# Turning the last two first blocks on quarters of the array, and converting v one head at a time

## The chip, the cores and the metric

The kernel runs on one core of a Trainium2 chip. The metric is the device time of one execution in microseconds (us), lower is better. Engine names are those of the profile: PE is the matrix engine, PEld its weight loads, DVE the vector engine, ACT the scalar engine, POOL the GpSimd engine, SP the engine that here only issues DMAs.

## What is computed

Attention with a forgetting gate over 8 batches, 8 heads, 576 positions and 64 numbers a head, and behind it a feed-forward layer on the 4,608 tokens:

```python
scores = scale * q @ k.T                                  # per batch and head, 576 x 576
cum    = cumsum(log(clip(f, 1e-4, 1)))                    # per batch and head
scores = where(causal, -1e9, scores + cum[:, None] - cum[None, :])
attn   = softmax(scores)
x      = (attn @ v), heads side by side                   # 4608 x 512
h      = x @ w_in                                         # 4608 x 2048
out    = (h * sigmoid(h)) @ w_out                         # 4608 x 512
```

The gate's factor of a key is put onto v: a row of v times its weight, with a column of ones beside it, so that one product gives both the numerator and the denominator of the softmax.

## The kernel before

**Blocks.** The 576 positions of a sequence are cut into a *first block* (128 rows), a *rest* (three blocks of 128) and a *tail* (64 rows). All engines' orders are written out by hand: an engine runs its instructions in the order of the calls in the source.

**First blocks.** For each batch `b`, `load_qk0(b)` (POOL's DMA queue, line 134) brings q and k of the first 128 rows as bf16 into one tile `qkb`, two DMAs a batch, each over all 128 partitions (16 runs of 8 rows, times 8 heads). `turn0(b, i)` turns q (`i` = 0) or k (`i` = 1) so that the 64 numbers of a head lie on partitions: 16 products on PE (line 293) with the loaded numbers as weights, 128 rows by 64 columns of the array, and a selection matrix `sel` as the moving operand, into a PSUM tile `tp` of the pool `pbig` (four buffers, shared with `hp`, `po`, `dn`, `tx`). ACT copies the turned q out, DVE the turned k (line 300). `scores0`, `mask0`, `out0` and `back0` do the attention of the block; score tiles come from the pool `psc` (tag "sc", two buffers). The function `two_more(b)` does the batches 4 and 5, later 6 and 7, with feed-forward work between its steps.

**Feed-forward work.** `m1_chunk` is the first product (PE line 583 into `hp`, then ACT's tanh, line 591, and DVE's product, line 592, into `gt`), `m2_part` a quarter of a second product (line 628 into `po`, four products of 512 columns), `m2_rows` the same on halves of the array's rows (line 654). `step(kind)` issues the next one; kind 1 is a chunk, kind 2 a part. `fill(us)` issues steps until about so many microseconds of PE time are used. They are what PE does between the attention's steps.

**Rest and tail.** 32 pairs of heads, `n` = 0 to 31, four a batch. q and k come in as float32 (`load_qk`, SP's queue; the second half of k straight into `qkb` by POOL's queue, line 160), `cast_qk` makes them bf16 on POOL (lines 409 and 413), `transposes(n)` turns them by a transposing DMA into `qkT` (SP's queue, line 443), `scores(n, c)` (PE line 475, then ACT's exponentials) and `mask`/`mask_tail` (DVE lines 492 and 498) follow, and `attend(n)` (PE lines 522 and 531) multiplies with v. `qkT` has four buffers. `turn(n)` casts, loads and turns three and four pairs ahead.

**v.** `load_v(b, c)` brings a block of v for all 8 heads as float32 into `vf`. `convert_v(b, c)` on POOL (line 429) multiplies it by the weights and writes bf16 into `vp`: one `tensor_tensor` over 8 heads of 65 columns (520), with the weight broadcast along the columns; the tail (`c` = 3) is two of 260 columns on 64 partitions. It is called for the next batch, `c` = 0 and 1 at the third pair of a batch, `c` = 2 and 3 at the fourth, after that pair's casts and k loads in POOL's order.

**The order around the change.** After the first four first blocks, POOL's order is: small fills, `load_w_out` 0 and 1, `convert_v0` of 4 and 5 (which wait for their v), `load_w_out` 2 and 3, `load_qk0` 6 and 7, `load_v0` 6 and 7, then the casts of the pairs. SP starts the loads of the pairs when `w_out`'s second quarter has landed. PE does `two_more(4)`, eleven steps in a written order of kinds, `fill(2.2)`, `two_more(6)`, `fill(4.2)`, and then the loop over the pairs.

Of the kernel before, what the change touches and what calls it, by code (L numbers as in the profile page):

```python
# [9 lines left out]
ALU = mybir.AluOpType  # L10
FP32 = mybir.dt.float32
BF16 = mybir.dt.bfloat16
P = 128
# [5 lines left out]
def kernel(  # L19
# [10 lines left out]
    nc = tc.nc  # L30

    B, H, S, D = q.shape
    DM, DFF = moe_w_in.shape
    BH = B * H
    NCC = DM // P
    NFC = DFF // P
    NP = H // 2
    SM = 512
    ST = S - SM
    NM = SM // P  # L40
    NR = NM - 1
# [6 lines left out]
    RUN = 8  # L48
    NRUN = P // RUN
    assert D == 64 and S == 576 and DM == H * D and NP == NCC and B == 8  # L50
    assert NRUN * H == P
    scale = 1.0 / float(D) ** 0.5

    ctx.enter_context(tc.manual_schedule(engines=set(ORDERED)))
# [1 line left out]
    const = ctx.enter_context(tc.tile_pool(name="const", bufs=1))  # L56
    stage = ctx.enter_context(tc.tile_pool(name="stage", bufs=1))
    conv = ctx.enter_context(tc.tile_pool(name="conv", bufs=6))
    qktp = ctx.enter_context(tc.tile_pool(name="qktp", bufs=4))
# [8 lines left out]
    psc = ctx.enter_context(tc.tile_pool(name="psc", bufs=2, space=bass.MemoryType.PSUM))  # L68
# [2 lines left out]
    w_in_bf = const.tile([P, NCC, DFF], BF16, name="w_in_bf")  # L71
    w_out_bf = const.tile([P, NFC, DM], BF16, name="w_out_bf")
    w_bf = const.tile([P, NM + 1, BH], BF16, name="w_bf")
    ident_bf = const.tile([P, P], BF16, name="ident_bf")
    sel = const.tile([P, 2, D], BF16, name="sel")
    ident_f = const.tile([BH, BH], FP32, name="ident_f")
    tri = const.tile([P, P], BF16, name="tri")
    trit = const.tile([P, 2, ST], BF16, name="trit")
# [3 lines left out]
    junk = const.tile([1, 16], BF16, name="junk")  # L82
    kT0 = [const.tile([P, NP, P], BF16, name=f"kT0_{b}") for b in range(B)]
    v0 = [const.tile([P, H, D + 1], BF16, name=f"v0_{b}") for b in range(B)]
    vps = [const.tile([P, NM, H, D + 1], BF16, name=f"vp_{i}") for i in range(2)]
    uts = [const.tile([P, NM + 1, 3, ST], BF16, name=f"ut_{i}") for i in range(4)]
    vfs = [const.tile([P, H, D + 1], FP32, name=f"vf_{i}") for i in range(4)]

# [41 lines left out]

    def load_qk0(b):
        t = conv.tile([P, 2, RUN * D], BF16, name="qkb", tag="qkb")
        for i, src in enumerate((q, k)):
            nc.gpsimd.dma_start(
                out=t[:, i, :],
                in_=src[b, :, 0:P, :].rearrange("h (r c) d -> r h (c d)", c=RUN),
            )
        qk0[b] = t

    def load_v0(b):  # L140
# [62 lines left out]
    def load_w_out(i):  # L203
        c0, c1 = i * NFC // WQ, (i + 1) * NFC // WQ
        nc.gpsimd.dma_start(
            out=w_out_bf[:, c0:c1, :],
            in_=moe_w_out[c0 * P : c1 * P, :].rearrange("(fc p) m -> p fc m", p=P),
        )
# [76 lines left out]
    def turn0(b, i):  # L285
        src = qk0[b]
        if i == 0:
            qT0[b] = qktp.tile([P, NP, P], BF16, name="qT0", tag="qT0", bufs=2)
        dst, evac = ((qT0[b], nc.scalar.copy), (kT0[b], nc.vector.tensor_copy))[i]
        tp = pbig.tile([P, NP, NRUN, RUN], FP32, name="tp", tag="big")  # L290
        for c in range(RUN):
            for j in range(2):
                nc.tensor.matmul(  # L293
                    tp[j * D : (j + 1) * D, :, :, c].rearrange("p a r -> p (a r)"),
                    lhsT=src[:, i, c * D : (c + 1) * D],
                    rhs=sel[:, j, :],
                    start=True,
                    stop=True,
                )
        evac(  # L300
            out=dst[:, :, :].rearrange("p a t -> p (a t)"),
            in_=tp[:, :, :, :].rearrange("p a r c -> p (a r c)"),
        )
# [43 lines left out]
    def convert_v0(b):  # L347
        nc.gpsimd.tensor_tensor(
            out=v0[b][:, :, :],
            in0=vf0.pop(b)[:, :, :],  # L350
            in1=w_bf[:, 0, b * H : (b + 1) * H, None].to_broadcast([P, H, D + 1]),
            op=ALU.mult,
        )
# [64 lines left out]
    def convert_v(b, c):  # L418
        vbf[b] = vps[b % 2]
        if c < NR:  # L420
            parts = [(slice(0, P), slice(0, P), slice(0, H), slice(0, H))]
        else:
            parts = [
                (slice((1 - i) * ST, (2 - i) * ST), slice(ST, P), slice(0, NP), slice(i * NP, (i + 1) * NP))
                for i in range(2)
            ]
        for ro, r, ho, h in parts:
            w = w_bf[r, c + 1, b * H + h.start : b * H + h.stop, None]
            nc.gpsimd.tensor_tensor(  # L429
                out=vbf[b][ro, c, ho, :],  # L430
                in0=vst[b][c][r, h, :],
                in1=w.to_broadcast([r.stop - r.start, h.stop - h.start, D + 1]),
                op=ALU.mult,
            )
# [71 lines left out]
    def attend(n):  # L506
        b, p = divmod(n, NP)
        if p % 2 == 0:
            xqs[n // 2] = xqp.tile([P, NGR, 2, D], BF16, name="xr", tag="xr", bufs=3)
        xq = xqs[n // 2]  # L510
        u, ut = us.pop(n), uts[n % 4]
        dn = pbig.tile([P, NGR, D + 1], FP32, name="dn", tag="big")

        def vals(kb, i):
            h = head(p, i)
            return v0[b][:, h, :] if kb == 0 else vbf[b][:, kb - 1, h, :]

        for i in range(2):
            for c in range(1, NM):
                for kb in range(c + 1):  # L520
                    o = AT[c, kb]
                    nc.tensor.matmul(  # L522
                        dn[:, i * NR + c - 1, :],
                        lhsT=u[:, i, o : o + P],
                        rhs=vals(kb, i),
                        start=(kb == 0),
                        stop=(kb == c),
                    )
        for j in range(2 * NM + 1):
            kb, i = (j % NM, j // NM) if j < 2 * NM else (NM, 0)  # L530
            nc.tensor.matmul(  # L531
                dn[:, NGR - 1, :],
                lhsT=ut[:, kb, i : i + 2, :].rearrange("p i t -> p (i t)"),
                rhs=vals(kb, i) if kb < NM else vbf[b][:, NR, p, :],
                start=(j == 0),
                stop=(j == 2 * NM),
            )
        rec = recp.tile([P, NGR], FP32, name="rec", tag="rec")
        nc.vector.reciprocal(out=rec[:, :], in_=dn[:, :, D])
        nc.vector.tensor_tensor(  # L540
            out=xq[:, :, p % 2, :],
            in0=dn[:, :, 0:D],
            in1=rec[:, :, None].to_broadcast([P, NGR, D]),
            op=ALU.mult,
        )
# [208 lines left out]
    def fill(us_, least=0, ends=(0, 0)):  # L754

        left = us_ + at["left"]
        kinds = plan(left)
        kinds += [0] * (least - len(kinds))
        if any(ends) and kinds:
            if 2 not in kinds:  # L760
                kinds[0] = 2
            n1, n2 = len(kinds) - kinds.count(2), kinds.count(2)
            e0 = 1 if ends[0] else 0
            e1 = 1 if ends[1] and n2 > e0 else 0
            inner = n2 - e0 - e1
            n = n1 + inner
            mid = [2 if (x + 1) * inner // n > x * inner // n else 1 for x in range(n)]
            if inner and mid[-1] == 2 and e1 and not e0:
                mid = mid[::-1]
            kinds = [2] * e0 + mid + [2] * e1  # L770
        for k in kinds:
            t = step(k)
            if t is None:
                at["left"] = 0.0
                return
            left -= t / 1000
        at["left"] = left
# [48 lines left out]
    for i in range(2):  # L826
        r = slice((1 - i) * ST, (2 - i) * ST)
        nc.gpsimd.tensor_copy(out=trit[r, i, :], in_=tri[r, r])
    for t in uts:
        nc.gpsimd.memset(t[:, 0:NM, 1, :], 0.0)  # L830
    load_w_out(0)
    load_w_out(1)
    convert_v0(4)
    convert_v0(5)
    load_w_out(2)
    load_w_out(3)
    load_qk0(6)
    load_qk0(7)
    load_v0(6)
    load_v0(7)  # L840
# [11 lines left out]
    cast_qk(1)  # L852
    transposes(1)

    def two_more(b):
        for x in range(2):
            turn0(b + x, 0)
            turn0(b + x, 1)
        fill(1.2, 2)
        for x in range(2):  # L860
            scores0(b + x)
            mask0(b + x)
        fill(2.6 if b == 4 else 3.4, 3)
        out0(b)
        fill(0.6, 1)
        out0(b + 1)
        fill(0.8, 2)
        back0(b, on_act)
        fill(0.6, 1)
        back0(b + 1, on_act)  # L870
        if b == 4:
            open2["w"] = True
            step(2)
        else:
            fill(0.6, 1)
# [1 line left out]
    fill(5.9)  # L877
    two_more(4)
    ready.add(1)
    for kind in (1, 1, 2, 1, 1, 2, 1, 1, 1, 1, 2):  # L880
        assert step(kind) is not None
    at["left"] = 0.0
    begin[M1[at["m1"]][0]] = (M1[at["m1"]][1], at["m2"])
    fill(2.2)
    two_more(6)
    ready.add(2)
    store(len(stores))
# [6 lines left out]
    for c in range(NM):  # L894
        convert_v(0, c)
    fill(4.2)

# [193 lines left out]
```

## Time and profile before

| what | value |
|---|---|
| median of 3 runs | 339.35 us (338.65 to 339.97) |
| the profiled execution's own time | 341.14 us |
| its span, first to last instruction | 339.4 us, 1.7 us less |
| PE busy | 326.7 us, 96% of the span |
| DVE, ACT, POOL busy | 200.5, 217.2, 139.5 us |
| granted PE clock | 0.999 |

The profile is one execution, and its time is 1.8 us over the median of the runs. In the timeline a row is start, duration, engine, line, operation, output<-inputs, shapes and count; what stands in brackets is how long the engine was idle ahead of it and who ended that. The chain is read from the top down in order of time: each row waited for the row above it.

### The profile page before, as it was taken

To read this page: it belongs to the slowest core of one execution; us is meant where nothing else is said; L and a number is where in the kernel's file an instruction comes from. 1 tells how busy PE (TensorE), PEld (TensorE's weight loads), DVE (VectorE), ACT (ScalarE), POOL (GpSimd) and SP (SyncE) were. 2 spreads that over 40 slices of the span, in tenths; PEclk is the share of its full clock that TensorE was granted. 3 is DMA by queue.
4 is the path that set the end of the run, shared out by engine and by line. 5 is a ranking of instruction groups with operands and counts; after the bars stand their busy time and mean duration, and the time that the engine had idled before them with its cause. 6 is when DMAs were issued, how large, how long until landed. Compare 5 with 4: busy or idle time off the path is not lost.

```text
span 339.4 us, 10334 instructions
## 1 busy us (share of the span) xinstructions
PE 326.7 (96%) x4268; PEld 229.2 (68%) x4292; DVE 200.5 (59%) x435; ACT 217.2 (64%) x385; POOL 139.5 (41%) x223
## 2 busy tenths in 40 slices
PE   7999999999999999999999997999999999999995
PEld 3745566798786767758857894867676676555654
DVE  4668745369568467565656965886673557344330
ACT  5767546687777577758748792866776486344431
POOL 8894426574764664464474352628060000000000
PEclk9999999999999999999999999999999999999999
DMA  8999999999999998997999789959973110001012
GB/s 155 187 189 220 180 215 164 241 171 172 182 188 170 168 186 158 194 190 150 181 179 165 147 148 147 156 115 188 151 108 87 53 38 33 34 33 59 34 62 63
DMA packets 144703, 48.01 MB, mean 141 GB/s; under 512 B 133328, under 2 KB 139728, under 8 KB 144656
## 3 DMA queue, kind: packets, MB, share of 16 engines
q1 hardware_dynamic: 115088, 36.60, 56.9%
q0 software_dynamic: 29408, 10.62, 27.0%
q8 instruction: 33, 0.54, 0.7%
q10 hardware_dynamic: 160, 0.13, 0.2%
q14 instruction: 14, 0.11, 0.1%
HBM read 36.85 MB, written 9.44 MB: 136 GB/s over the span
## 4 chain that ended last, share of the span: by engine, by line
PE 85%; DMA 6%; DVE 4%; POOL 2%; issue 1%; ACT 1%; SPq 1%; POOLq 0%
PE hp L583 33%; PE po L628 20%; PE pr L654 15%; PE sc L475 6%; PE dn L522 5%; DMA vf<-in_v_dram 3%; PE dn L531 2%; DMA qkb<-in_k_dram 1%; PE tp L293 1%; DVE gt L592 1%; DMA qf<-in_q_dram 1%; DVE ut L498 1%; DVE u L343 1%; SPq L443 1%; POOL vp L429 1%
## 5 line engine op out<-in xcount | busy, mean ns | idle before, releaser
L591 ACT ACTIVATE th<-hp 128x384 bf16<-128x384 f32 (+2 forms) x208 | 96.5, 468 | 75.0 <-PE hp L583 68.8
L592 DVE SCALAR_TENSOR_TENSOR gt<-th,hp 128x384 bf16<-128x384 bf16 (+2 forms) x208 | 107.5, 523 | 54.3 <-ACT th L591 44.3
L583 PE MATMUL hp<-x,w_in_bf 128*128 128x384 bf16 (+2 forms) x701 | 120.6, 321 | 0.7 <-DVE gt L592 0.4
L583 PEld LDWEIGHTS <-w_in_bf 128*128 128x128 bf16 x832 | 79.0, 98 | 50.2 <-issue 3.7
L486 ACT ACTIVATE u<-sc 128x1024 bf16<-128x1024 f32 (+1 forms) x96 | 74.3, 811 | 6.9 <-PE sc L475 6.9
L628 PE MATMUL po<-w_out_bf,gt 128*128 128x512 bf16 (+1 forms) x316 | 74.1, 368 | 1.4 <-DVE gt L592 0.2
L654 PE MATMUL pr<-w_out_bf,gt 64*128 64x256 bf16 x1024 | 61.4, 269 | 0.0
L409 POOL CAST qkb<-qf 128x384 bf16<-128x384 f32 x32 | 17.3, 542 | 88.9 <-DMA qf<-in_q_dram 88.3
L654 PEld LDWEIGHTS <-gt 64*128 64x128 bf16 x1024 | 51.2, 94 | 3.9
L628 PEld LDWEIGHTS <-gt 128*128 128x128 bf16 x336 | 32.2, 98 | 27.4 <-issue 0.3
L160 POOL DMA_DIRECT2D qkb<-in_k_dram x56 | 43.9, 786 | 0.8 <-issue 0.7
L429 POOL TENSOR_TENSOR vp<-vf,w_bf 128x520 bf16<-128x520 f32 (+1 forms) x40 | 36.5, 915 | 14.0 <-DMA vf<-in_v_dram 11.9
L638 ACT ACTIVATE osb<-po 128x512 f32<-128x512 f32 (+1 forms) x21 | 12.1, 577 | 26.5 <-PE po L628 26.5
L475 PE MATMUL sc<-qkT 64*128 64x128 bf16 (+1 forms) x640 | 28.2, 206 | 0.4 <-DMA qkT<-qkb 0.3
L492 DVE TENSOR_TENSOR u<-u,tri 128x768 bf16<-128x768 bf16 x32 | 20.2, 631 | 13.5 <-ACT u L486 13.5
L475 PEld LDWEIGHTS <-qkT 64*128 64x128 bf16 x640 | 20.3, 94 | 7.6 <-issue 4.7
L480 ACT ACTIVATE ut<-sc 128x640 bf16<-128x640 f32 x32 | 22.4, 701 | 3.0 <-PE sc L475 2.5
L522 PEld LDWEIGHTS <-u 128*128 128x128 bf16 x576 | 20.6, 97 | 3.1
L522 PE MATMUL dn<-vp,u 128*128 128x65 bf16 x384 | 21.8, 193 | 0.0
L540 DVE TENSOR_TENSOR xr<-dn,rec 128x448 bf16<-128x448 f32 x32 | 20.0, 625 | 1.1
L522 PE MATMUL dn<-v,u 128*128 128x65 bf16 x192 | 20.0, 194 | 0.0
L665 DVE COPY fence<-pr 128x1 f32<-128x1 f32 x16 | 2.5, 158 | 28.0 <-PE pr L654 28.0
(70 smaller groups left out, 243.4 us busy)
## 6 DMA issues: line engine op xcount, KB each, us to landing
out_dram<-osb SPq DMA_DIRECT2D x32, 256.0 KB, 2.9
vf<-in_v_dram SPq DMA_DIRECT2D x26, 256.0 KB, 5.1
qf<-in_q_dram SPq DMA_DIRECT2D x64, 96.0 KB, 3.3
qkb<-in_k_dram POOLq DMA_DIRECT2D x56, 48.0 KB, 4.0
w_in_bf<-in_moe_w_in_dram POOLq DMA_DIRECT2D x4, 512.0 KB, 6.8
w_out_bf<-in_moe_w_out_dram POOLq DMA_DIRECT2D x4, 512.0 KB, 9.1
vf<-in_v_dram POOLq DMA_DIRECT2D x6, 256.0 KB, 9.6
qkb<-in_q_dram POOLq DMA_DIRECT2D x8, 128.0 KB, 4.9
```

The costliest lines, as they stand in the source:

```text
L160: nc.gpsimd.dma_start(out=t2[:, NR + 1 : NX, j * D : (j + 1) * D], in_=k[b, head(p, j), P:SM, :].rearrange("(c p) d -> p c d", p=P),)
L429: nc.gpsimd.tensor_tensor(out=vbf[b][ro, c, ho, :], in0=vst[b][c][r, h, :], in1=w.to_broadcast([r.stop - r.start, h.stop - h.start, D + 1] ...
L475: nc.tensor.matmul(sc[:, i, o : o + q1 - q0], lhsT=kt, rhs=t[r, q0:q1], start=True, stop=True)
L480: nc.scalar.activation(out=ut[:, :, 0:3:2, :].rearrange("p k i t -> p i k t"), in_=sc[:, :, T0 : T0 + (NM + 1) * ST].rearrange("p i (k t) ...
L486: nc.scalar.activation(out=u[:, :, c * SM : c * SM + w], in_=sc[:, :, 0:w], func=ACT.Exp, scale=scale)
L492: nc.vector.tensor_tensor(out=x, in0=x, in1=tri[:, None, None, :].to_broadcast([P, 2, NR, P]), op=ALU.mult)
L522: nc.tensor.matmul(dn[:, i * NR + c - 1, :], lhsT=u[:, i, o : o + P], rhs=vals(kb, i), start=(kb == 0), stop=(kb == c),)
L583: nc.tensor.matmul(hp[:, :], lhsT=w_in_bf[:, cc, fc * P : (fc + 1) * P], rhs=xcols(g, cc), start=(cc == 0), stop=(cc == NCC - 1),)
L591: nc.scalar.activation(out=th[:, :], in_=hp[:, :], func=ACT.Tanh, scale=0.5)
L592: nc.vector.scalar_tensor_tensor(out=gt[:, fc, :], in0=th[:, :], scalar=1.0, in1=hp[:, :], op0=ALU.add, op1=ALU.mult,)
L628: nc.tensor.matmul(po[:, :], lhsT=gt[:, fc, tb * P : (tb + 1) * P], rhs=w_out_bf[:, fc, m0:m1], start=(fc == 0), stop=(fc == NFC - 1),)
L654: nc.tensor.matmul(pos[g, tb][y], lhsT=gt[r, fc, tb * P : (tb + 1) * P], rhs=w_out_bf[r, fc, y * DM // 2 : (y + 1) * DM // 2], start=(half ...
```

## The change

It has these parts.

1. `load_qk0` of batches 6 and 7 uses four DMAs of 64 partitions in place of two of 128: q lies on the lower 64 partitions, k on the upper, with the heads 0 to 3 and 4 to 7 side by side.
2. `turn0_quarters` turns these two batches. A product uses 64 rows and 64 columns of the array, 64 moving columns as before; the four that follow each other lie on the four quarters. There are 64 products for the two batches, as before. q and k go into one two-bank tile of the score pool (`psc`) in place of two tiles of `pbig`. The copies by ACT and DVE are of the same size; both now follow all 32 products of a batch.
3. A selection matrix `selh` is made by two DVE copies, and float32 weights `w_f` by one POOL copy.
4. `load_qk0(6)` moves in POOL's order ahead of `convert_v0(4)` and so ahead of the second half of `w_out`.
5. The steps between `two_more(4)` and `two_more(6)` have two chunks more, `fill(2.2)` becomes `fill(1.8)`, and a chunk follows `fill(4.2)`.
6. `convert_v` for batches 2 to 7 is, for each head, one `tensor_scalar` of 65 columns with a weight per partition: 8 instructions for a block in place of one, 8 for the tail in place of two. Batches 0 and 1 stay as they were. `vp` gets a flat layout.

```diff
@@ load_qk0
-        for i, src in enumerate((q, k)):
-            nc.gpsimd.dma_start(
-                out=t[:, i, :],
-                in_=src[b, :, 0:P, :].rearrange("h (r c) d -> r h (c d)", c=RUN),
-            )
+        for z, src in enumerate((q, k)):
+            if b < 6:
...
+                continue
+            for i in range(2):
+                nc.gpsimd.dma_start(
+                    out=t[z * D : (z + 1) * D, i, :],
+                    in_=src[b, i * NP : (i + 1) * NP, 0:P, :].rearrange(
+                        "a (r c) d -> r a (c d)", c=RUN
+                    ),
+                )
@@ convert_v
+            if b > 1:
+                for x in range(h.stop - h.start):
+                    z = b * H + h.start + x
+                    nc.gpsimd.tensor_scalar(
+                        out=vbf[b][ro, c * H + ho.start + x, :],
+                        in0=vst[b][c][r, h.start + x, :],
+                        scalar1=w_f[r, c, z : z + 1],
+                        scalar2=None,
+                        op0=ALU.mult,
+                    )
+                continue
@@ POOL's order
+    nc.gpsimd.tensor_copy(out=w_f[:, :, :], in_=w_bf[:, 1 : NM + 1, :])
     for t in uts:
         nc.gpsimd.memset(t[:, 0:NM, 1, :], 0.0)
     load_w_out(0)
     load_w_out(1)
+    load_qk0(6)
     convert_v0(4)
     convert_v0(5)
     load_w_out(2)
     load_w_out(3)
-    load_qk0(6)
     load_qk0(7)
@@ new
+    def turn0_quarters(b):
+        qT0[b] = qktp.tile([P, NP, P], BF16, name="qT0", tag="qT0", bufs=2)
+        sc = psc.tile([P, 2, NP, NRUN, RUN], FP32, name="tq", tag="sc")
+        for c in range(RUN):
+            for j in range(2):
+                for i in range(2):
+                    r = slice(i * D, (i + 1) * D)
+                    nc.tensor.matmul(
+                        sc[j * D : (j + 1) * D, i, :, :, c].rearrange("p a r -> p (a r)"),
+                        lhsT=qk0[b][r, j, c * D : (c + 1) * D],
+                        rhs=selh[r, :],
+                        start=True,
+                        stop=True,
+                    )
...
@@ between two_more(4) and two_more(6)
-    for kind in (1, 1, 2, 1, 1, 2, 1, 1, 1, 1, 2):
+    for kind in (1, 1, 2, 1, 1, 1, 1, 2, 1, 1, 1, 1, 2):
...
-    fill(2.2)
+    fill(1.8)
     two_more(6)
...
     fill(4.2)
+    step(1)
```

More of the change, by code (lines that the diff above doesn't have):

```diff
@@ L50 @@
     assert D == 64 and S == 576 and DM == H * D and NP == NCC and B == 8
-    assert NRUN * H == P
+    assert NRUN * H == P and NRUN * NP == D
     scale = 1.0 / float(D) ** 0.5
@@ L73 @@
     w_bf = const.tile([P, NM + 1, BH], BF16, name="w_bf")
+    w_f = const.tile([P, NM, BH], FP32, name="w_f")
     ident_bf = const.tile([P, P], BF16, name="ident_bf")
     sel = const.tile([P, 2, D], BF16, name="sel")
+    selh = const.tile([P, D], BF16, name="selh")
     ident_f = const.tile([BH, BH], FP32, name="ident_f")
@@ L84 @@
     v0 = [const.tile([P, H, D + 1], BF16, name=f"v0_{b}") for b in range(B)]
-    vps = [const.tile([P, NM, H, D + 1], BF16, name=f"vp_{i}") for i in range(2)]
+    vps = [const.tile([P, NR * H + NP, D + 1], BF16, name=f"vp_{i}") for i in range(2)]
     uts = [const.tile([P, NM + 1, 3, ST], BF16, name=f"ut_{i}") for i in range(4)]
@@ L132, in load_qk0 @@
         t = conv.tile([P, 2, RUN * D], BF16, name="qkb", tag="qkb")
-        for i, src in enumerate((q, k)):
-            nc.gpsimd.dma_start(
-                out=t[:, i, :],
-                in_=src[b, :, 0:P, :].rearrange("h (r c) d -> r h (c d)", c=RUN),
-            )
+        for z, src in enumerate((q, k)):
+            if b < 6:
+                nc.gpsimd.dma_start(
+                    out=t[:, z, :],
+                    in_=src[b, :, 0:P, :].rearrange("h (r c) d -> r h (c d)", c=RUN),
+                )
+                continue
+            for i in range(2):
+                nc.gpsimd.dma_start(
+                    out=t[z * D : (z + 1) * D, i, :],
[3 more added lines that the diff above has]
+                )
         qk0[b] = t
@@ L427, in convert_v @@
         for ro, r, ho, h in parts:
+            if b > 1:
[9 more added lines that the diff above has]
+                continue
             w = w_bf[r, c + 1, b * H + h.start : b * H + h.stop, None]
             nc.gpsimd.tensor_tensor(
-                out=vbf[b][ro, c, ho, :],
+                out=vbf[b][ro, c * H : c * H + ho.stop, :],
                 in0=vst[b][c][r, h, :],
@@ L515, in vals @@
             h = head(p, i)
-            return v0[b][:, h, :] if kb == 0 else vbf[b][:, kb - 1, h, :]
+            return v0[b][:, h, :] if kb == 0 else vbf[b][:, (kb - 1) * H + h, :]
         for i in range(2):
@@ L533, in attend @@
                 lhsT=ut[:, kb, i : i + 2, :].rearrange("p i t -> p (i t)"),
-                rhs=vals(kb, i) if kb < NM else vbf[b][:, NR, p, :],
+                rhs=vals(kb, i) if kb < NM else vbf[b][:, NR * H + p, :],
                 start=(j == 0),
@@ L853 @@
     transposes(1)
+    for z in range(2):
+        r = slice(z * D, (z + 1) * D)
+        nc.vector.tensor_copy(
+            out=selh[r, :].rearrange("p (a r) -> p a r", a=NP),
+            in_=ident_bf[r, r].rearrange("p (r a) -> p a r", a=NP),
+        )
+    def turn0_quarters(b):
[11 more added lines that the diff above has]
+                        stop=True,
+                    )
+        for i, (dst, evac) in enumerate(
+            ((qT0[b], nc.scalar.copy), (kT0[b], nc.vector.tensor_copy))
+        ):
+            evac(
+                out=dst[:, :, :].rearrange("p a t -> p (a t)"),
+                in_=sc[:, i, :, :, :].rearrange("p a r c -> p (a r c)"),
+            )
     def two_more(b):
         for x in range(2):
-            turn0(b + x, 0)
-            turn0(b + x, 1)
+            if b == 4:
+                turn0(b + x, 0)
+                turn0(b + x, 1)
+            else:
+                turn0_quarters(b + x)
         fill(1.2, 2)
```

## Prediction

> **What bounds the kernel now.** The page's first part says that PE is busy for 96% of the span, so I looked for the places where PE stands still, and for what a faster PE would run into. The busy table and the waits come first.
>
> ```profile
> PE 326.7 (96%) x4268; PEld 229.2 (68%) x4292; DVE 200.5 (59%) x435; ACT 217.2 (64%) x385; POOL 139.5 (41%) x223
> ```
>
> ```profile
> POOL qkb L409 <- DMA qf<-in_q_dram: 88.3, 21, 10.2
> ...
> PE hp L583 <- DVE gt L592: 2.6, 3, 2.2
> ...
> PE sc L475 <- DMA qkT<-qkb: 0.3, 1, 0.3
> ```
>
> In the second, the table of waits, the numbers are total, times and longest, in us. POOL has 88.3 us of waiting for data. PE itself waited long only once: 2.2 us for DVE's product. The timeline finds that place at 203 us:
>
> ```profile
> 202.02 1.56 POOL L160 DMA_DIRECT2D qkb<-in_k_dram  x2
> ...
> 202.99 2.78 DVE L498 TENSOR_TENSOR ut<-ut,trit 128x128 bf16<-128x128 bf16 x1
> ...
> 203.60 2.08 POOL L429 TENSOR_TENSOR vp<-vf,w_bf 128x520 bf16<-128x520 f32 x2
> ...
> 205.69 1.40 DVE L592 SCALAR_TENSOR_TENSOR gt<-th,hp 128x256 bf16<-128x256 bf16 x4
> 206.15 0.60 PE L583 MATMUL hp<-xt,w_in_bf 128*128 128x256 bf16 x4 [2.24 <-DVE gt L592]
> ```
>
> The tail's mask (L498) takes 0.22 us where POOL is quiet. Here it takes 2.78 and ends as POOL's two conversions of v end; the products behind it on DVE are late, the `hp` buffers are not freed, and PE stops for 2.24 us. At 234.88 the same mask takes 2.44 us beside the next such pair, but PE has 2.54 us of second products in hand and loses nothing. So conversions keep DVE out, and one such meeting costs time.
>
> The chain that ended last shows the other tight place:
>
> ```profile
> 74.44 0.71 ACT ut L480
> ...
> 75.96 3.60 DMA qf<-in_q_dram
> ...
> 80.45 2.45 SPq L443
> 82.89 0.04 issue
> 82.94 4.83 DMA vf<-in_v_dram
> ...
> 87.83 1.06 POOL vp L429
> ```
>
> It leaves PE at 74 us and comes back at 90.5 through loads, a transposing DMA, v's load and batch 1's conversions. The windows table gives a summed DMA packet time of 1.35 of the engines' time from 76.7 to 90.7 us. PE's wait for `qkT` of pair 5 at 86.87 is 0.28 us, that for `vp` at 90.51 is 0.18: both are just met.
>
> **Quarters (parts 1 to 3).** The 64 turning products take 2.01 us in the chain (47.45), two at a time: 32 pairs, 55 ns a pair from start to start. Four at a time would be 16 groups; at 55 ns a group that is 0.9 us, and without more overlap it stays 2.0. No row shows quarters. The nearest is L654: halves of the rows do 32 products of 256 columns in 1.75 us, 55 ns each, where the whole array (L583, 8 in 0.87) needs 109: two halves overlap fully. I take 1.0 us saved, bounds 0 and 1.1. [...]
>
> ACT's two copies (0.59 each) and DVE's (0.69) start 0.45 us later against a product train that ends 1.0 earlier, while PE has a part and a chunk (1.3 us) to do; without that cover the scores would wait some 0.5 us. The score pool's two buffers were last read by `out0(5)` at 36.9, ten us before. `selh` is two small DVE copies (a 128x64 copy, L232, takes 0.24), 0.5 us, in 1.49 us in which DVE waits for the first tanh at 20.3; if they came behind it, the four `hp` buffers would carry most of it. `w_f` is a POOL cast of 256 columns: from L409 and L413 (451 and 239 ns from start to start for 384 and 128 columns) 0.13 + 0.83 ns a column, 0.35 us.
>
> **The saving's way to the end.** In the written order two chunks more (8 products, 0.87 us) come ahead of the first pair's scores, and eight fewer at the end of the second quad. So pairs 0 to 3 stay where they are to 0.1 us, and pair 4 comes 0.9 earlier. Two products later PE meets `qkT` of pair 5 and batch 1's `vp`, both on the DMA chain above, which does not move with PE. So the wait of 0.28 becomes about 1.1, and the 1.0 us is eaten there. I count 0.1 gained; 0.9 if the chain comes earlier too, −0.4 if `w_f` and the four extra DMAs push the chain (it starts with `w_out`'s second quarter, issued 0.35 us later behind transfers that take 9.8 and 11.1 us to land).
>
> **POOL's queue (part 4).** `load_qk0(6)` is now four issues of some 0.55 us (L134), 2.2 us, where POOL was idle for 4.42 us waiting for v of batch 4 at 29.75: free; without that cover 2.2 us on every later load. Four issues for batch 7 stand where four stood, so `load_v0` keeps its place. In the queue of transfers batch 6 (landings 0.87 us apart, 1.75 together) passes `w_out` 2 and 3: they land near 40.5 and 43.2 in place of 38.8 and 41.5, and are read at 41.2 plus 0.87 (two chunks more ahead) and 44.0 plus 0.87: 1.5 us of room each, nothing lost. Were half-width DMAs to take twice as long, this room would be gone, and 0.3 us lost.
>
> **Conversions (part 6).** Per block 8 instructions in place of one of 1.06 us. 65 columns by the casts' line are 0.19 us, the nearest row since they too read one tensor; twice that, 0.35, is my upper bound, for the weight's read. I take 0.25: 2.0 us a block, and 2.0 for the tail in place of 1.4. A batch costs 3 × 0.94 + 0.6 = 3.4 us more, six batches 20 us, against POOL's 88.3 us of waiting. Behind them on POOL are the next casts and k loads; `qkT` of pairs 10 to 31 lands 4.5 us or more before its scores (pair 13 the least). The tight one is batch 2's second half: it starts at 109.88, and PE reads `vp` from 113.99 on, the tail's at 114.9. At 0.25 it is done at 113.9; above 0.4 PE would wait.
>
> What DVE waits for: two-input conversions that followed without a gap let DVE's mask in only after both. Two casts that followed without a gap let it in between:
>
> ```profile
> 74.18 0.50 POOL L409 CAST qkb<-qf 128x384 bf16<-128x384 f32 x1 [0.84 <-DMA qf<-in_q_dram]
> 74.31 0.78 DVE L492 TENSOR_TENSOR u<-u,tri 128x768 bf16<-128x768 bf16 x1
> 74.64 0.62 POOL L413 CAST qkb<-qktf 128x128 bf16<-128x128 f32 x1
> ```
>
> L492 takes 0.55 alone, so it waited 0.23 and the second cast waited for it (0.62 for 0.29). The short conversions are nearest to these. Then the mask at 203 waits for one of them, 0.25 us, and of its old delay of 2.56 us, 0.32 was already covered: PE's 2.24 us go, and nothing is late in their place, since from there on the transposes lead by 13 us and more. [...]
>
> **The sum** against the profiled execution: 341.14 − 2.24 + 0.05 − 0.1 = 338.85, 0.67% less. That on the median of 339.35 is 337.1.
>
> **The rivals.**
>
> *The run holds the port (slower).* The eight or sixteen short conversions behave like the pair at 203: DVE is let in only when POOL's queue runs empty. For: L498 was kept out by conversions that began after it. Against: the casts. It decides where a run of sixteen lasts over 2.08 us, 0.13 us each, which even the lower bound exceeds. At 203 the mask waits for 16 × 0.25 = 4.0 in place of 2.08: 1.9 more. At 235 the 2.54 us of cover are overrun by as much, some 0.6 to 1.9. Together about 2.5: 341.8.
>
> *The stall is not in the timed runs.* The profiled execution is 1.8 us over the median, nearly what the meeting at 203 cost, and a shift of POOL by 1 us avoids it. For: that number, and the runs' spread of 1.3. Against: POOL at 203 follows PE's own pace through `qkT`'s buffers, so the meeting should recur. Then only the turn's 0.1 is left, as it is if another meeting replaces this one: 339.2.
>
> *The DMA chain moves too.* The stores and loads ahead of it wait partly for ACT's copies, which come earlier, so pair 5 keeps the 0.9: 336.2. Against: DMA is at its limit there.
>
> That the quarters don't overlap changes none of these times by over 0.1, since that gain is not kept.
>
> **How the numbers follow.** Chances: forecast 0.40, stall absent or replaced 0.26, run holds the port 0.22, chain moves 0.12. About 0.5% (1.7 us) can be told from no change here; the limits are 337.65 and 341.05. The forecast's own range, 336.7 to 338.2, lies three quarters under the first. Faster: 0.29 + 0.11 = 0.40; slower: 0.18 of the run plus 0.02 of the second rival (a new meeting that costs) = 0.20; the rest 0.40. The range reaches from the moved chain's 336.0 to 341.8, and leaves out half of the third case and little below.
>
> **What would show it.** Right: 16 groups of four in about 0.9 us near 47.6; L498 and L492 nowhere over 1.1 us from 95 on; no PE gap of over 1 us near 203; PE's wait at pair 5 near 1 us. Wrong: a mask as long as a run of conversions; conversions over 0.4 us each with PE waiting for `vp` at 114; PE waiting for `w_out` at 42 to 45.

## The result, and the profile after

The changed kernel takes 341.78 us (median of 22 runs, 339.88 to 343.71); the kernel before, in as many runs, 339.35 (338.26 to 341.44). The ratio is 1.0068, interval 1.0049 to 1.0087: slower by 0.68%, 2.4 us. The forecast was 0.67% faster, and the result lies at the upper edge of the range. The profiled execution of after took 342.84 us (span 341.1), 1.1 over its median.

The page's busy times:

```profile
PE 330.1 (97%) x4292; PEld 229.1 (67%) x4292; DVE 195.1 (57%) x437; ACT 217.2 (64%) x385; POOL 200.6 (59%) x390
```

POOL went from 139.5 to 200.6 us, 61 us more where some 20 were forecast. The table of waits (total, times, longest) tells where PE met that:

```profile
POOL qkb L420 <- DMA qf<-in_q_dram: 39.4, 17, 8.3
...
PE dn L553 <- POOL vp L442: 2.2, 1, 2.2
...
PE sc L497 <- DMA qkT<-qkb: 0.8, 1, 0.8
```

POOL's wait for q has fallen from 88.3 to 39.4. PE's long wait is a new one: for `vp`, written by the short conversions (L442). The stall for `gt` is gone. The timeline of after at batch 2:

```profile
110.34 8.29 POOL L442 TENSOR_SCALAR vp<-vf,w_f 128x65 bf16<-128x65 f32 x16
...
117.06 0.19 PE L553 MATMUL dn<-vp,ut 128*128 128x65 bf16 x1 [2.18 <-POOL vp L442]
...
117.09 4.03 PE L650 MATMUL po<-w_out_bf,gt 128*128 128x512 bf16 x12
```

The second half of batch 2's conversions starts about where it did (109.88 before), but lasts 8.29 us in place of 2.66. PE has finished the other products of the tail at 114.88 and waits 2.18 us. The third row shows a second cost: twelve products of 512 columns take 4.03 us; the same twelve take 2.59 at 174.10. The windows table (length, busy time of PE, PEld, DVE, ACT and POOL with counts, granted clock, DMA share, GB/s) gives the reason:

```profile
114.00:116.00 2.00, 0.88 (x26) 0.79 (x27) 0.70 (x3) 1.72 (x3) 1.71 (x4) 1.00 0.45 92
116.00:118.00 2.00, 0.94 (x6) 0.47 (x6) 0.68 (x2) 0.00 (x0) 1.72 (x4) 1.00 0.27 61
118.00:120.00 2.00, 2.00 (x7) 0.72 (x6) 0.28 (x2) 0.00 (x0) 1.85 (x5) 0.60 0.00 0
120.00:122.00 2.00, 2.00 (x26) 1.39 (x25) 0.00 (x0) 0.00 (x0) 2.00 (x5) 0.55 0.90 103
```

For 3.4 us behind the wait, from 118.4 to 121.8, the clock is half (0.50): 1.7 us lost. The chain that ended last now goes through POOL twice:

```profile
81.54 2.22 SPq L465
83.81 3.92 DMA vf<-in_v_dram
87.80 1.06 POOL vp L451
...
103.14 4.74 DMA qf<-in_q_dram
110.34 4.02 POOL vp L442 x8
117.25 3.87 PE po L650 x12
```

The first three rows are the old tight place at batch 1, the last three the new one at batch 2. And what stands in after where the old stall was, at 203 us:

```profile
203.32 0.57 POOL L420 CAST qkb<-qf 128x384 bf16<-128x384 f32 x1
...
203.80 0.23 DVE L520 TENSOR_TENSOR ut<-ut,trit 128x128 bf16<-128x128 bf16 x1 [0.27 <-ACT ut L502]
```

The mask takes 0.23 us and PE has no wait there. But this is not the old meeting: the conversions that met the mask in before, batch 6's first two blocks, begin here only at 211.78, and the mask meets two casts. The masks that do run beside those conversions, at 217.86 and 218.72, take 0.56 and 0.23 us. The turn on quarters, from the timeline and from the groups (mean ns of one behind the busy time) the two forms of the short conversion:

```profile
48.19 1.09 PE L892 MATMUL tq<-selh,qkb 64*64 64x64 bf16 x64
```

```profile
L442 POOL TENSOR_SCALAR vp<-vf,w_f 128x65 bf16<-128x65 f32 x144 | 64.1, 465 | 0.6
...
L442 POOL TENSOR_SCALAR vp<-vf,w_f 64x65 bf16<-64x65 f32 x48 | 22.9, 477 | 3.9
```

The 64 products start four at a time, a group every 55 ns: 0.85 us from the first start to the last, 1.84 before. The short conversions follow each other 0.42 us from start to start, on the tail's 64 partitions 0.53.

### The profile page after: what moved, and what is told of

Same layout as the page of the kernel before. It is cut to its first block, busy times and chain, and to the rows that moved or that the text cites. A ratio compares the mean times of both kernels' runs of the same rounds, so it can differ in the third digit from the quotient of the medians.

```text
span 341.1 us, 10515 instructions
## 1 busy us (share of the span) xinstructions
PE 330.1 (97%) x4292; PEld 229.1 (67%) x4292; DVE 195.1 (57%) x437; ACT 217.2 (64%) x385; POOL 200.6 (59%) x390
## 4 chain that ended last, share of the span: by engine, by line
PE 83%; DMA 5%; POOL 4%; DVE 3%; ACT 2%; SPq 1%; issue 1%; POOLq 0%
PE hp L605 32%; PE po L650 21%; PE pr L676 14%; PE sc L497 6%; PE dn L544 5%; DMA qf<-in_q_dram 3%; PE dn L553 2%; POOL vp L442 2%; PE tp L304 2%; DMA qkb<-in_k_dram 2%; DMA vf<-in_v_dram 1%; DVE gt L614 1%; DVE u L354 1%; POOL vp L451 1%; SPq L465 1%
## 5 line engine op out<-in xcount | busy, mean ns | idle before, releaser
L442 POOL TENSOR_SCALAR vp<-vf,w_f 128x65 bf16<-128x65 f32 (+1 forms) x192 | 87.0, 468 | 4.6
L650 PE MATMUL po<-w_out_bf,gt 128*128 128x512 bf16 (+1 forms) x336 | 78.9, 373 | 0.2 <-DVE gt L614 0.2
L420 POOL CAST qkb<-qf 128x384 bf16<-128x384 f32 x32 | 16.7, 521 | 39.9 <-DMA qf<-in_q_dram 39.4
L561 DVE RECIPROCAL rec<-dn 128x7 f32<-128x7 f32 x32 | 6.5, 203 | 21.0 <-PE dn L553 21.0
```

Of the source, the lines that this page charges most:

```text
L442: nc.gpsimd.tensor_scalar(out=vbf[b][ro, c * H + ho.start + x, :], in0=vst[b][c][r, h.start + x, :], scalar1=w_f[r, c, z : z + 1], scalar2 ...
L650: nc.tensor.matmul(po[:, :], lhsT=gt[:, fc, tb * P : (tb + 1) * P], rhs=w_out_bf[:, fc, m0:m1], start=(fc == 0), stop=(fc == NFC - 1),)
```

## The experiments

My theory after the first profile: the short conversions of batch 2 are too slow for their place, and all else of the change is neutral or a gain. Rivals: the quarters or the moved loads cost time; the old stall was an accident of one execution, so that its disappearance pays nothing; the clock behind the wait is the main cost.

**Parts 1 to 5 without part 6.** Edit of after, run twice:

```diff
-            if b > 1:
+            if b > 7:
```

> The changed kernel with part 6 undone: all blocks of v converted by one instruction over 8 heads, the quarters, the moved loads and the step order kept. Theory (short conversions make PE wait for v of batch 2 at 114 us, and the idle time lowers PE's clock after it): the 2.2 us wait at 114 and the clock of 0.5 at 118 to 121.6 are gone, some 3.9 us; the meeting of mask and conversions near 203 may return with up to 2.2 us. Time 338.5 to 340, not above the kernel before. Rival (the quarters and the moved loads cost): the time stays near 341.8.

> Part 6 undone once more, to narrow the interval of parts 1 to 5 alone (0.9937 to 1.0001 the first time). If the saved turning time is all eaten at pair 5, the ratio is within 0.999 to 1.001; if half a us or more is kept, it is 0.996 to 0.998.

Measured: 338.3 us, ratio 0.9969 (0.9937 to 1.0001), and 338.12, ratio 0.9968 (0.9938 to 0.9997). So quarters and moved loads cost nothing; they gain about 0.3%, 1.1 us. In both traces PE waits longer for `qkT` of pair 5 (1.1 and 1.5 us), as the prediction had it. The waits of the first:

```profile
PE sc L497 <- DMA qkT<-qkb: 1.1, 1, 1.1
...
PE dn L553 <- POOL vp L451: 0.5, 1, 0.5
```

**Part 6 without the rest.** The kernel before, with `convert_v`, the layout of `vp` and the copy `w_f` of after:

```diff
+            if b > 1:
+                for x in range(h.stop - h.start):
+                    nc.gpsimd.tensor_scalar(
...
```

> The kernel before with part 6 alone: conversions head by head for batches 2 to 7, all else in the old order. Theory: PE waits about 2 us for v of batch 2 at 114, the clock falls for some 3.4 us behind it, the stall at 203 is gone: 341 to 342.5. Rival: 339.5 or less, the loss being in parts 1 to 5.

Measured: 342.7 us, ratio 1.0088 (1.0062 to 1.0114). The whole loss is in part 6. In its trace PE waits 1.11 us for `vp` at batch 2 and 1.64 at batch 3, with the clock at 1.00 behind both.

**Short conversions from batch 3 on.** After with batch 2 converted as before, run twice; and the same conversions on the kernel before (old turn, old order of loads):

```diff
-            if b > 1:
+            if b > 2:
```

> The changed kernel with head by head conversion from batch 3 on alone, so batch 2's four blocks in one instruction each (the tail in two). Theory: no wait for v at 114, no clock below 1, no stall at 203; POOL is still 0.42 us an instruction. About 338 (3.9 less than the changed kernel's 341.8). If long occupation of POOL itself is what costs, it stays over 340.5.

> Head by head from batch 3 on with parts 1 to 5, once more: near 338.0 (ratio 0.993 to 0.997) if the first result holds; the same as with whole blocks (the run beside it) if the short conversions give nothing of their own.

> The kernel before with head by head conversion from batch 3 on: parts 1 to 5 undone, batch 2 whole. If what the variant with conversion from batch 3 on gained (338.0) comes from the quarters and the moved loads, this one is not faster than the kernel before (339 to 340); if it comes from the short conversions' milder hold on the ports, this one too is near 338.

Measured: after with `b > 2` 338.02 us, ratio 0.9951 (0.9929 to 0.9973), and 337.4, ratio 0.9944 (0.9924 to 0.9965); with the old turn 338.18, ratio 0.9967 (0.9945 to 0.9989). So the one condition is worth 1.0068 − 0.9951 = 1.2%, 4.0 us; on the old turn 1.0088 − 0.9967, the same. After with `b > 2` beats both kernels, by half a per cent against before. Its interval overlaps that of parts 1 to 5 alone.

**Both kernels once more**, one execution each:

> The kernel before once more, for a second trace. If the meeting of mask and conversions near 203 recurs, PE waits 1.5 to 2.5 us there again; if it was an accident, there is no wait over 0.5 us and the span is near 337.

> The changed kernel once more, for a second trace. The wait for v at 114 (1 to 2.5 us) should be there again, at batch 3 (143) up to 1.6; the lowered clock only where PE stood long enough.

Measured: before 337.67 us (span 335.9), after 340.97 (span 339.2). This execution of before is faster than any of its timed runs (the lowest is 337.72). It has no stall: its mask came ahead of the conversions, and nothing kept it out. Of the 3.5 us between the two spans of before the stall is 2.4: from the scores of pair 21 to those of pair 22 PE takes 14.88 us with it and 12.49 without. Nearly all of the rest lies ahead of pair 6.

```profile
202.02 0.21 DVE L498 TENSOR_TENSOR ut<-ut,trit 128x128 bf16<-128x128 bf16 x1
...
202.62 1.04 POOL L429 TENSOR_TENSOR vp<-vf,w_bf 128x520 bf16<-128x520 f32 x1
```

After waits twice, and its clock stays at 1.00. From its timeline:

```profile
115.17 0.19 PE L553 MATMUL dn<-vp,ut 128*128 128x65 bf16 x1 [1.64 <-POOL vp L442]
...
137.87 8.15 POOL L442 TENSOR_SCALAR vp<-vf,w_f 128x65 bf16<-128x65 f32 x16
...
144.45 0.19 PE L553 MATMUL dn<-vp,ut 128*128 128x65 bf16 x1 [1.64 <-POOL vp L442]
```

1.64 + 1.64 = 3.28 us, and the spans differ by 3.3. That the two agree so well is in part chance. PE's pace from one pair's scores to the next differs between the two traces at few places: up to pair 6 after is 0.40 us ahead, from pair 9 to 10 it loses 1.80 and from pair 13 to 14 again 1.80, and 0.13 later. So the two waits, with 0.16 us behind each, are more than the whole loss. The second is inherited. With batch 2 converted whole (the first of the `b > 2` kernels) the same set of batch 3 lasts as long but starts 4.5 us earlier, and PE reads without a wait:

```profile
133.37 8.23 POOL L442 TENSOR_SCALAR vp<-vf,w_f 128x65 bf16<-128x65 f32 x16
...
141.40 0.28 PE L553 MATMUL dn<-vp,ut 128*128 128x65 bf16 x4
```

**Short conversions for batch 6 alone**, the one at 203 us, on the kernel before (`if b == 6`):

> The kernel before, with batch 6 alone (the one converted at 203 us) head by head, all else as before. Theory: the meeting near 203 cannot last there, and batch 6 is long ahead of PE, so nothing else changes: where the meeting recurs in the timed runs this is 1 to 2.2 us faster than the kernel before (337 to 338.2); if the stall of 203 was an accident of the one profiled execution, it is the same (339).

Measured: 339.04 us, ratio 0.9991 (0.9975 to 1.0007). Its mask at 203.54 took 0.28 us; it was over before the first short conversion began at 204.21, so this trace has no meeting at all. The runs gained nothing that can be told from noise, and by the interval 0.25% (0.85 us) at most. So the stall of the first profile, 2.24 us, was not in the usual run; in some it may have been.

**PE kept busy in the wait.** After, with nine products whose result is not used (`keep_warm`) in `attend` ahead of the tail's last one of pair 8:

```diff
+            if n == 8 and kb == NM:
+                keep_warm(9)
```

> The changed kernel with 9 more products of 512 zero columns (a tile that nobody reads) on PE in the attention of pair 8, just ahead of the product that waits for v: PE is busy for about 1.9 us of the 2.2 us wait. It computes the same. If idle time of PE is what lowers the clock, the clock stays at 1.0 at 118 and pair 10 starts 1.7 us earlier than in the changed kernel, time about 340.1. If the clock falls for another reason (load before it, time), it falls all the same and the time stays at 341.8.

Measured: 340.77 us, ratio 1.0048 (1.0022 to 1.0074), an interval that overlaps that of after. In its trace PE has no wait at batch 2 and the clock is 1.00 from 118 to 122, but it halves at another place instead, again behind time in which PE stood still (1.1 us for v and 0.5 us, at 16 to 18 us):

```profile
16.00:18.00 2.00, 0.81 (x14) 0.58 (x13) 1.06 (x4) 1.09 (x3) 2.00 (x4) 1.00 0.80 109
18.00:20.00 2.00, 1.82 (x8) 0.71 (x7) 0.69 (x4) 0.37 (x1) 2.00 (x4) 0.63 1.19 185
20.00:22.00 2.00, 2.00 (x7) 0.65 (x5) 0.69 (x1) 0.60 (x1) 1.18 (x3) 0.52 1.20 185
```

From pair 9's scores to pair 10's PE takes 14.90 us here. In after it took 16.94 in the first trace and 14.76 in the second, where the clock stayed at 1.00 without the extra products; with batch 2 converted whole it takes 12.96. So keeping PE busy does not settle whether idle time lowers the clock, and the place of a fall is seen only in the profiled execution. The runs of after say more: in seven of its 22 the mean granted clock is 0.992 to 0.995, and their median is 342.88 us (mean 342.65); in the other 15 it is 0.999 or 1.000, and their median is 341.41 (mean 341.61). Where it comes the half clock costs some 1.0 to 1.5 us, and without it after is still 2.1 us over before. A clock of 0.993 to 0.995 comes in 8 of 79 runs of before too, whose conversions of batch 2 are whole. The clock is a share of the loss, not the main one.

**A constant for the weight.** After with `scalar1=0.75`:

> The changed kernel with the constant 0.75 in place of the weight per partition in the short conversions, so the gate's factor is left out for the blocks after the first of batches 2 to 7. If the weight's read makes the 0.42 us of a short conversion, it falls to about 0.19 (the casts' line) and the wait at 114 goes; if it is the instruction's own start, it stays over 0.35 and so does the wait.

This kernel leaves out the gate's factor for those blocks; its instructions are as many and as large. Measured, in one execution: 337.77 us. From start to start a short conversion takes 0.335 us in place of 0.42 (the groups give durations):

```profile
L442 POOL TENSOR_SCALAR vp<-vf 128x65 bf16<-128x65 f32 x144 | 51.3, 391 | 0.4
...
L442 POOL TENSOR_SCALAR vp<-vf 64x65 bf16<-64x65 f32 x48 | 18.5, 386 | 3.4
```

The weight's read is 0.085 us of it; the other 0.335 is there without it, where the casts' line gave 0.19 for 65 columns. So both expected causes have a part, the instruction's own cost the larger. What either consists of no run here shows. PE's waits for `vp` shrink to 0.36 and 0.34 us.

## Why the prediction was wrong

**The step that failed: the size of a short conversion.** "I take 0.25 us", with bounds of 0.19 and 0.35 from the casts' line, measured 0.42 on whole blocks and 0.53 on the tail, above the upper bound. The row was the nearest by its count of inputs, but a cast of 128 or 384 columns says little of another instruction with 65. Doubling the casts' figure for the upper bound (twice 0.19 is 0.38, not 0.35) was too little as well. The prediction's own condition, "above 0.4 PE would wait", then held word for word: PE needs the eight conversions of the block and the first five of the tail, 8 × 0.42 + 5 × 0.53 = 6.0 us from 110.34 on, thus 116.4 at best, where 114.9 was its due time. Two conversions that overlapped masks of DVE, 0.66 and 0.79 us in place of 0.44, added most of the rest. That 341.78 still lies within the stated range is luck: the range's top, 341.8, was the time of the rival in which the run holds the port, and that did not happen.

**Only one set was costed.** The prediction looked at batch 2's second half and, "behind them on POOL", at `qkT`. It did not ask when POOL would reach batch 3's set. That set had 8 us in the first profile of before (133.96 to 141.99); in the second profile of after it came 3.9 us later (137.87) and lasted 8.15 us, and PE, there at 142.81, waited 1.64 us for it.

**A stall of one execution was credited to all.** The 2.24 us at 203 are absent in after, but it is not shown that they went by the mechanism that was forecast: the meeting itself had moved, and before's second execution lacks the stall with nothing changed. What was forecast of the masks beside short conversions did hold elsewhere (0.66 us at most in after). The rival "the stall is not in the timed runs" (0.26) was right on this point: taking the meeting away alone gave 0.9991. Crediting every run with what one execution showed was the fault. Why that second execution, at 337.67 us, is 1.7 us under the median of before is open. The rival's time, 339.2, missed too, for the first reason.

The reading of the stall had a gap as well. The mask of 203 began 0.61 us ahead of the first conversion and takes 0.22 alone, so conversions cannot have kept it out from its start. POOL was then still issuing a transfer (L160, until 203.58). So it did not find POOL idle, and that conversions which began after it kept it out, as the rival of the run has it, does not follow from this row.

**The sum with the measured terms.** For the profiled execution: 338.85, the forecast, + 2.18 for the wait + 1.7 for the half clock = 342.7; measured 342.84. For the second executions, without stall and half clock: 337.67 + 3.28 = 340.95; measured 340.97, with the chance in it that was said above.

**The half clock** was in no case of the prediction, and what brings it no run here settles. In after's first trace it came behind a wait of 2.18 us, with PE busy for 1.82 us of the four from 114 to 118; in the trace with PE kept busy it came behind waits of 1.1 and 0.5 us. After's second execution had two waits of 1.64 us and no fall. So the length of a single wait does not tell where it comes.

**The turn** came out as forecast in itself, 1.0 us saved. "I count 0.1 gained" was too low: alone, parts 1 to 5 gave 0.3%, about 1 us. The arrival of pair 5's `qkT` varies between executions (from 85.0 to 87.1 us in the traces). In after's second execution it comes at 85.1, and of 1.0 us gained on before's second execution up to pair 4 only 0.25 is lost again by pair 6; in the first trace of parts 1 to 5 alone it comes at 86.6, and all is lost. That is the rival of the moving chain, in part; that early arrivals make the 0.3% of the runs is argued, not shown.

**What held:** the masks (none over 0.86 us from 95 on, and in after none beside a short conversion over 0.66, so the rival of the run that holds the port falls; its "port", and the "ports" of one expectation, are the author's picture, and the traces show only who was late and by how much); no wait for `w_out`; the moved loads free in POOL's idle time; PE's wait at pair 5, 0.85 us, in the profiled execution.

One of the prediction's chances was also worked out wrongly: of its range of 336.7 to 338.2, 63% lies under 337.65 if it is evenly filled, not three quarters. That changes nothing in the outcome.

Why short conversions from batch 3 on gain 0.3% in the runs is shown only in part. Other meetings of a mask with whole conversions exist: in both traces of parts 1 to 5 alone the mask of the next such pair of conversions is held, for 2.60 us where it takes 0.21. The first of them:

```profile
232.57 2.60 DVE L520 TENSOR_TENSOR ut<-ut,trit 128x128 bf16<-128x128 bf16 x1
```

It costs PE 0.26 us: from pair 25's scores to pair 26's these two take 13.17 and 13.16 us, the two kernels with `b > 2` 12.90 and 12.91. That is under 0.1%; what else the runs gain is open.

## What to carry to other kernels

Eight small instructions took 8 × 0.42 = 3.4 us here in place of a large one's 1.06, and only a row of the same instruction at a like size would have told it; without one, the upper bound has to reach to where the schedule breaks. When an engine in the background slows down, follow its queue through every later due time, not only the tightest: lateness that isn't made up arrives at the next one. And a stall that the profile shows once is a forecast's gain only as often as it occurs; a second profiled execution would have shown that here.

## What was not expected of the hardware

In after, a mask of DVE is hardly held up by a short conversion that began before it (by 0.11 us at most; in two of the `b > 2` traces one mask each took 0.77 us); rather the conversion that overlaps it takes longer. The answer for the line of the short conversions in after (shortest, median and longest, in ns) shows it:

```profile
L442 POOL TENSOR_SCALAR vp<-vf,w_f x192: 439/444/837, 99.6 to 261.3; 128x65 bf16<-128x65 f32 x144, 64x65 bf16<-64x65 f32 x48
```

Each of the 14 that take over 0.5 us overlaps a mask of 0.55 us: ten begin within it, four up to 0.04 us ahead of it. The masks keep their 0.55 to 0.66 and 0.22 to 0.30 us. So short instructions on POOL turn the collision round here: it is POOL that is late, by up to 0.4 us a mask.

The long holds by whole conversions have a common start. All four masks that took 2.4 us or more (202.99 and 234.88 in before, 232.57 and 231.80 in parts 1 to 5 alone) began while POOL was issuing a transfer of k, with two whole conversions right behind it. The issue alone seldom holds a mask: of 175 masks that begin within such an issue from 58 us on, in all thirteen traces, 151 take at most 0.06 us longer than alone. What decides it no run here shows.
